# The opening of a fused DFT and gated-MLP kernel: one load queue for x, norm columns turned on the matmul engine, first weight folds moved ahead

## The chip, the core and the metric

The kernel runs on one core of a Trainium2 chip. The core has a matmul engine (TensorE, "PE" in the profile; its weight loads are shown apart as "PEld"), three engines for elementwise work (VectorE "DVE", ScalarE "ACT", GpSimd "POOL") and a synchronisation engine ("SP") that does little but issue transfers. 16 DMA engines move data between HBM and the core's memory (SBUF); transfers can be issued from SP, ACT and POOL, and each of these has a queue of its own. The matmul engine writes to PSUM, 2 KB banks per partition that DVE and ACT read and no transfer can reach. Everything is fp32, and a fp32 matmul instruction shows in the profile as two passes: 8 matmuls are listed as "x16".

The metric is the device time of one execution in microseconds.

## What is computed

```python
def _attn_ref(x):                       # x: (8, 3008, 256)
    X = np.fft.fft(x, axis=1)
    X = np.fft.fft(X, axis=2)
    return X.real

def _moe_ref(x, w_in, w_out):           # x: (24064, 256), w_in: (256, 2048), w_out: (2048, 256)
    h = x @ w_in
    g = h * np.cos(h)
    return g @ w_out
```

The output is `_moe_ref` of the real part of the 2-D transform.

## The kernel before

**The work.** 3008 = 47 x 64, so the transform along the sequence is done in two halves. The first half (`first_half`) multiplies by a 47-point DFT, for 4 columns i of the 64-column grid and their mirror columns at a time: eight chunks c = 0..7 per batch. Its results go to DRAM (`store_z`), come back turned (`load_z`), and the second half (`second_half`) multiplies by the other DFT and yields a group g of up to 256 tokens. The transform along the 256 channels is folded into `w_in`: `fold_weights(e, n)` multiplies 512 columns of `w_in` by the cosine (e = 0) or sine (e = 1) matrix, and `keep_fold` writes the result to `WC` or `WS`. One row of the sine fold, the "norm row", is kept apart by `keep_row` (`nrow[n]`); it is needed as a column, 128 values on 128 partitions, in `wn`.

**The steady state.** 8 batches x 6 groups x 8 pairs of hidden tiles make 384 steps. A step s has a `seed` (ACT writes `wn` column x `nb` + 0.25 into the PSUM tile H), two matmul groups `mm1(s, 0)` and `mm1(s, 1)` on top of it, rounding and sine on ACT, products on DVE, and 7 matmuls `mm2`. Steps are interleaved with a lag of 3 (`LAG`). `nb` is the group's norm row spread over 128 partitions; for all groups but the first it is made by two transfers on SP, `nd<-pq` (L530) and `nb<-nd` (L531), and the seeds of that group wait for it.

**The opening** (everything before the loop at L1018) is what the change is about. It is written out by hand: engines run their instructions in program order, and each of SP's, ACT's and POOL's transfers is issued in program order too.

- `load_x(p, c0, c1, side)` (L189-209) loads part of batch 0's x. Half p = 0 feeds chunks 0 to 3, p = 1 chunks 4 to 7; side 0 are the columns, side 1 the mirror columns. Each call is three transfers (16, 16 and 15 rows of the 47). Side 0 goes by SP; side 1 of p = 0 and the first half of side 1 of p = 1 go by ACT's queue, the rest by SP. One single column goes by POOL.
- SP and ACT share eight semaphores for their transfers in turn, so a transfer waits until the one eight before it has landed.
- `keep_busy(8, "H", 512)` (L904) runs 8 matmuls on constant data while x is on its way.
- `fold_chunk` (L297) makes sum and difference of x and its mirrored channels on DVE, with a small copy of channel 0 (L302) before them, in two buffers `xf0`. `middle(b, p)` (L335) transforms channel 128 for all 16 columns of half p at once; `DIRECT` = 7 is a chunk that PE folds itself, with twice the matmuls.
- The chunks run in the order 0, 1, 2, 3, 4, 5, 7, 6. The sine fold n = 0 is put before chunk 4 (L913-915), the cosine fold n = 0 and folds n = 1 after the last chunk, then `second_half(0, 0)`.
- `store_z(0, c, 0)` sends the near part of a chunk to DRAM: chunks 0 to 3 from POOL, later ones from SP, two of them from ACT. `load_z(0, 0)` waits for all eight chunks' near parts.
- `send_wn(n)` and `take_wn(n)` (L608-615) turn the norm row into a column: a transfer from SBUF to DRAM and one back, both on POOL's queue. Columns of n = 0 belong to steps 0 and 1 of each group (in the first group these use `seed_first`, a matmul on the row itself, instead); n = 1 serves steps 2 and 3, n = 2 steps 4 and 5, n = 3 steps 6 and 7.
- Loads of batch 1's x follow on SP (21 transfers, L180) and on POOL (7 transfers); then SP loads `xz` (L185) and only then comes to `nd` and `nb` of group 1.

The lines that the steps below touch: L302/L303 (chunk folds), L339/L346 (middle), L455/L440/L443 (first half), L577 (weight folds), L590/L594 (their copies by ACT), L598 (norm row), L610/L613 (norm column through DRAM), L627 (`keep_busy`), L660 (`seed`), L676 (`seed_first`), L690 (`mm1`), L780 (`mm2`), L507/L518/L522 (second half and its copies).

Of the kernel before, what the change touches and what calls it, by code (L numbers as in the profile page):

```python
# [11 lines left out]
FP = mybir.dt.float32  # L12
# [122 lines left out]
def kernel(  # L135
# [119 lines left out]
    nc.sync.dma_start(out=LCS, in_=LCS_dr.ap())  # L255
    nc.vector.memset(xs[0][:, 0:2048], 0.0)
# [12 lines left out]
    load_w(0)  # L269
# [27 lines left out]
    def fold_chunk(b, c, e):  # L297
# [3 lines left out]
        if e == 0:  # L301
            nc.vector.tensor_copy(out=fv[:, 0, :, 0], in_=xv[:, :, 0])  # L302
# [32 lines left out]
    def middle(b, p):  # L335
        xm = xs[p].rearrange("r (i d) -> r i d", d=ND)[0:XR, :, 128]
        pm = psum("pm", "M")[64:128, 0:XP]
        for i0, i1, q in ((0, 1, 2), (1, XP, 0)) if p == 0 else ((0, XP, 0),):
            nc.tensor.matmul(  # L339
                pm[:, i0:i1],  # L340
                lhsT=L[0:XR, 64 * q : 64 * q + 64],
                rhs=xm[:, i0:i1],
                start=True,
                stop=True,
            )
        nc.scalar.copy(out=mid[64:128, XP * p : XP * p + XP], in_=pm)  # L346
# [77 lines left out]
    def first_half(b, c):  # L424
# [3 lines left out]
        if c == 0:  # L428
            middle(b, 0)
# [70 lines left out]
    def second_half(b, g):  # L500
# [3 lines left out]
        pb = psum("pb")  # L504
        for q in range(4):
# [8 lines left out]
        pq = spool.tile([128, 512], FP, tag="pq", bufs=8, name="pq")  # L514
        pv = pq[:, 0 : 2 * T].rearrange("d (e t) -> d e t", e=2)
        bv = pb.rearrange("d (q e k) -> d e q k", q=4, e=2)
        if g == 0:
# [3 lines left out]
            edge = nc.scalar.copy if b else nc.vector.tensor_copy  # L521
            edge(out=pv[:, :, 192:225], in_=bv[:, :, 0, 0:33])  # L522
# [83 lines left out]
    wds = {}  # L606
# [96 lines left out]
    def dve_h(s):  # L703
        T = s.T
        s.h = spool.tile([128, 512], FP, tag="h", bufs=3, name="h")
        nc.vector.tensor_tensor(  # L706
# [221 lines left out]
    take_wn(1)  # L928
    fold(0, 1)
# [5 lines left out]
    for c in range(NCH):  # L935
# [6 lines left out]
    second_half(0, 0)  # L942
    combine_w2(2, 4)

    opening = {
        3: ((send_wn, 3), (take_wn, 3)),
# [9 lines left out]
    early = {3: (1, 3, "fft"), 5: (0, 3, "fft")}  # L956
# [12 lines left out]
    dve_h(s0)  # L969
# [8 lines left out]
    send_wn(2)  # L978
    take_wn(2)
# [10 lines left out]
    act_round(s1, 1)  # L990
    mm1(s2, 1)
# [17 lines left out]
    def beside(ins, ahead):  # L1009
        if ahead is not None:  # L1010
            tc.add_manual_dep(
                ins.ins,
                ahead.ins.name,
                mybir.DependencyInfo(mybir.DependencyClass.Sync, mybir.DependencyReason.DATA),
                reason="start with the PSUM reads",
            )

    for t in range(LAG, n + LAG + 1):  # L1018
        cur, prev, old, done = step(t), step(t - 1), step(t - 2), step(t - LAG)
        if cur:  # L1020
            mm1(cur, 0)
            act_e(cur)
            if t in early:
                fold(*early[t])
# [82 lines left out]
```

## Time and profile before

| | us |
|---|---|
| median of 3 runs | 1951.06 (1950.06 to 1951.55) |
| the profiled execution's own time | 1949.91 |
| its span, first to last instruction | 1948.1 |
| PE busy | 1929.5 |
| DVE busy | 1778.5 |
| ACT busy | 1528.7 |
| POOL busy | 397.8 |

The profile is of one execution; all its times are counted from the start of the span. The timeline lists instructions in order of time, those of one line merged: start, length, engine, line, operation, tiles written and read, count, and in brackets the idle time of the engine before it and what ended it. Times of a merged row reach from the first start to the last end. The view of windows gives, for a stretch, the busy time of each engine, the granted clock of PE (1.00 is full speed), the DMA engines' share and the GB/s moved. The chain of waits is followed back from the last instruction; 58% of it are L780 matmuls and 34% L690 matmuls.

### The profile page before, as it was taken

To read this page: it belongs to the slowest core of one execution; us is meant where nothing else is said; L and a number is where in the kernel's file an instruction comes from. 1 tells how busy PE (TensorE), PEld (TensorE's weight loads), DVE (VectorE), ACT (ScalarE), POOL (GpSimd) and SP (SyncE) were. 2 spreads that over 40 slices of the span, in tenths; PEclk is the share of its full clock that TensorE was granted. 3 is DMA by queue.
4 is the path that set the end of the run, shared out by engine and by line. 5 is a ranking of instruction groups with operands and counts; after the bars stand their busy time and mean duration, and the time that the engine had idled before them with its cause. 6 is when DMAs were issued, how large, how long until landed. Compare 5 with 4: busy or idle time off the path is not lost.

```text
span 1948.1 us, 30580 instructions
## 1 busy us (share of the span) xinstructions
PE 1929.5 (99%) x9546; PEld 1693.7 (87%) x9546; DVE 1778.5 (91%) x3343; ACT 1528.7 (78%) x2877; POOL 397.8 (20%) x468
## 2 busy tenths in 40 slices
PE   8999999999999999999999999999999999999998
PEld 3888899888998889988898888988889888898887
DVE  4899999999899998999989999899999999999998
ACT  3787878888788787888878788788877888788775
POOL 3322202222022211222112221122211222111101
PEclk9999999999999999999999999999999999999999
DMA  7321130012200121111211122111231100110000
GB/s 194 102 61 39 46 90 24 22 37 75 58 22 22 46 75 49 25 26 47 82 36 27 25 56 79 29 29 25 51 85 31 25 20 24 55 28 10 12 22 22
DMA packets 157804, 89.35 MB, mean 46 GB/s; under 512 B 106838, under 2 KB 152270, under 8 KB 155174
## 3 DMA queue, kind: packets, MB, share of 16 engines
q1 hardware_dynamic: 155331, 85.42, 16.6%
q10 hardware_dynamic: 1415, 1.27, 0.3%
q8 instruction: 76, 1.25, 0.3%
q0 software_dynamic: 896, 0.71, 0.2%
q14 instruction: 86, 0.70, 0.1%
HBM read 50.07 MB, written 37.28 MB: 45 GB/s over the span
## 4 chain that ended last, share of the span: by engine, by line
PE 96%; issue 1%; DMA 1%; DVE 1%; POOL 0%; SPq 0%; ACT 0%; ACTq 0%; DVEq 0%; POOLq 0%
PE M L780 58%; PE H L690 34%; PE pb L507 2%; PE pz L397 2%; DMA wn<-wd 0%; DMA xp<-in_x_dram 0%; PE pz L357 0%; DMA wd<-nrow 0%; SPq L887 0%; PE M L397 0%; POOL zd L487 0%; PE pz L385 0%; DVE r L735 0%; PE pz L455 0%; DVE S L746 0%
## 5 line engine op out<-in xcount | busy, mean ns | idle before, releaser
L780 PE MATMUL M<-S,VX 128*128 128x256 f32 (+1 forms) x2304 | 612.3, 375 | 0.0
L780 PEld LDWEIGHTS M<-S,VX 128*128 128x128 f32 x2304 | 437.8, 190 | 49.9
L721 ACT ACTIVATE r<-H 128x512 f32<-128x512 f32 (+1 forms) x384 | 226.1, 589 | 264.1 <-DVE h L706 262.5
L731 ACT ACTIVATE r<-r 128x1024 f32<-128x1024 f32 (+1 forms) x384 | 394.7, 1028 | 20.4 <-DVE r L725 16.2
L690 PE MATMUL H<-pq,WC 128*128 128x256 f32 (+1 forms) x1536 | 394.6, 379 | 2.0 <-ACT H L660 2.0
L690 PE MATMUL H<-pq,WS 128*128 128x256 f32 (+1 forms) x1536 | 389.6, 376 | 1.3 <-ACT ew L701 1.3
L780 PE MATMUL M<-r,w 128*128 128x256 f32 (+1 forms) x1536 | 387.7, 375 | 0.0
L660 ACT ACTIVATE H<-nb,wn 128x256 f32<-128x256 f32 (+1 forms) x764 | 362.0, 474 | 24.7 <-DMA wn<-wd 10.8
L706 DVE TENSOR_TENSOR h<-ew,H 128x512 f32<-128x512 f32 (+1 forms) x384 | 259.4, 676 | 101.9 <-PE H L690 69.1
L690 PEld LDWEIGHTS H<-pq,WC 128*128 128x128 f32 x1536 | 283.5, 190 | 52.8 <-ACT r L721 15.4
L780 PEld LDWEIGHTS M<-r,w 128*128 128x128 f32 x1536 | 300.1, 196 | 28.3 <-issue 0.9
L690 PEld LDWEIGHTS H<-pq,WS 128*128 128x128 f32 x1536 | 292.7, 191 | 35.6 <-ACT ew L701 2.3
L725 DVE SCALAR_TENSOR_TENSOR r<-r,H 128x512 f32<-128x512 f32 (+1 forms) x384 | 258.6, 674 | 34.5 <-ACT r L721 18.2
L701 ACT ACTIVATE ew<-H 128x512 f32<-128x512 f32 (+1 forms) x384 | 225.6, 588 | 53.1 <-PE H L690 44.4
L832 POOL TENSOR_TENSOR cb<-cb,mr 128x256 f32<-128x256 f32 (+3 forms) x188 | 158.0, 851 | 518.6 <-DVE S L756 484.0
L746 DVE TENSOR_TENSOR S<-r 128x512 f32<-128x512 f32 (+1 forms) x384 | 259.8, 676 | 0.1
L725 DVE SCALAR_TENSOR_TENSOR r<-r,h 128x512 f32<-128x512 f32 (+1 forms) x384 | 259.4, 676 | 0.0
L735 DVE SCALAR_TENSOR_TENSOR r<-H,r 128x512 f32<-128x512 f32 (+1 forms) x384 | 256.6, 668 | 2.3 <-ACT r L731 1.8
L735 DVE SCALAR_TENSOR_TENSOR r<-h,r 128x512 f32<-128x512 f32 (+1 forms) x384 | 258.4, 673 | 0.0
L721 ACT ACTIVATE r<-h 128x512 f32<-128x512 f32 (+1 forms) x384 | 236.0, 615 | 0.0
L316 POOL TENSOR_TENSOR xs<-xp 113x512 f32<-113x512 f32 x112 | 142.9, 1276 | 407.8 <-DVE S L756 405.3
L780 PE MATMUL M<-S,w 128*128 128x256 f32 (+1 forms) x768 | 225.5, 375 | 0.6 <-DVE S L756 0.6
(108 smaller groups left out, 1585.0 us busy)
## 6 DMA issues: line engine op xcount, KB each, us to landing
out_dram<-ob SPq DMA_DIRECT2D x728, 32.0 KB
xp<-in_x_dram SPq DMA_DIRECT2D x261, 56.0 KB
z<-zd SPq DMA_DIRECT2D x8, 1280.0 KB
zd<-zs SPq DMA_DIRECT2D x224, 40.0 KB
nb<-nd SPq DMA_DIRECT2D x40, 128.0 KB
zd<-zs SPq DMA_DIRECT2D x224, 8.0 KB
xp<-in_x_dram SPq DMA_DIRECT2D x54, 48.0 KB
xp<-in_x_dram SPq DMA_DIRECT2D x42, 49.0 KB
```

The lines of the kernel that those rows point to most:

```text
L316: return nc.gpsimd.tensor_tensor(out=xs2[e][0:XL], in0=xv[:, 0], in1=xv[:, 1], op=ALU.subtract if e else ALU.add,)
L660: nc.scalar.activation(out=s.H[:, u * T : u * T + T], in_=s.nb[:, 0:T], func=AF.Copy, bias=0.25, scale=wn[:, f : f + 1],)
L690: nc.tensor.matmul(s.H[:, u * T : u * T + T], lhsT=W[:, 128 * f : 128 * f + 128], rhs=s.pq[:, e * T : e * T + T], start=False, stop=True, ...
L701: nc.scalar.mul(out=s.ew[:, 0 : 2 * s.T], in_=s.H[:, 0 : 2 * s.T], mul=2.0)
L706: nc.vector.tensor_tensor(out=s.h[:, 0 : 2 * T].rearrange("p (u t) -> p u t", u=2)[:, :, ::-1], in0=s.ew[:, 0 : 2 * T].rearrange("p (u t) ...
L721: nc.scalar.activation(out=r, in_=h, func=AF.Copy, bias=BIG, scale=1.0)
L725: nc.vector.scalar_tensor_tensor(out=r, in0=r, scalar=-BIG, in1=h, op0=ALU.add, op1=ALU.subtract)
L731: nc.scalar.activation(out=r, in_=r, func=AF.Sin, bias=0.0, scale=SIN_SCALE)
L735: nc.vector.scalar_tensor_tensor(out=r, in0=h, scalar=-0.25, in1=r, op0=ALU.add, op1=ALU.mult)
L746: return nc.vector.tensor_tensor(out=sv[:, 0:2], in0=gv[:, 2:3].to_broadcast([128, 2, T]), in1=gv[:, 0:4:3], op=ALU.subtract,)
L780: nc.tensor.matmul(acc[key][m // 2][:, 256 * (m % 2) : 256 * (m % 2) + T], lhsT=w, rhs=a, start=first, stop=s.fp == 7, skip_group_check=True,)
L832: return nc.gpsimd.tensor_tensor(out=o, in0=a, in1=b, op=ALU.subtract if less else ALU.add)
```

## The change

It changes the opening in eleven places:

1. All of batch 0's x goes by SP's queue (the one single column stays on POOL). Side 0 is cut into pieces of 2 KB, no longer of 4 KB.
2. The load of `w_in`'s first 512 columns (`load_w(0)`) is issued right behind the constants, ahead of x.
3. `keep_busy` at the start is cut from 8 matmuls to 2; both folds n = 0 and the turning of their norm row follow at once, before chunk 0.
4. `send_wn` and `take_wn` are gone. `turn_row(n)` takes their place: four matmuls with the row's 128 values as weights and a single 1 as the moving operand, into a PSUM tile, and a copy of 4 columns to `wn` by DVE (n < 2) or ACT.
5. The channel-0 copies of the chunk folds leave DVE: chunks 0 to 3 on ACT, chunks 4 to 6 on POOL.
6. `middle` for the second half of x runs in two parts of 8 columns, before chunk 4 and before chunk 7.
7. The order of the chunks is 0, 1, 2, 3, 4, 7, 5, 6.
8. After the folds n = 1 and `turn_row(1)` one matmul on constant data is put ahead of `second_half(0, 0)`, and a half-length one behind it.
9. In `second_half(0, 0)` DVE's copy of the edge is placed behind the first of the four matmuls, ahead of ACT's copy.
10. `clear_later` (POOL's clearing of later buffers) comes after the first step's `dve_h` and waits for it.
11. `turn_row(2)` stands behind `mm1(s1, 1)`, `turn_row(3)` at step 4 behind `mm1(s4, 0)`.

POOL's program is then: stores of chunks 0 to 2, channel-0 copy of chunk 4, stores of chunk 3, channel-0 copies of chunks 5 and 6, the clearing, the 7 loads of batch 1's x.

```diff
     def load_x(p, c0, c1, side):
-        queue = nc.scalar if side and not c0 else nc.sync
...
-            load(nc.sync, 0, c0, c1, slice(i0 + c0, i0 + c1), max_dma_last_dim=4096)
+            load(nc.sync, 0, c0, c1, slice(i0 + c0, i0 + c1), max_dma_last_dim=2048)
...
-        load(queue, 3, c0 + skip, c1, slice(64 - i0 - c0 - skip, 64 - i0 - c1, -1))
+        load(nc.sync, 3, c0 + skip, c1, slice(64 - i0 - c0 - skip, 64 - i0 - c1, -1))
...
     nc.sync.dma_start(out=LCS, in_=LCS_dr.ap())
+    load_w(0)
...
-    load_w(0)
     for c0 in (0, XP // 2):
...
-    def clear_later():
-        nc.gpsimd.memset(xz, 0.0)
+    def clear_later(ahead):
+        beside(nc.gpsimd.memset(xz, 0.0), ahead)
...
-            nc.vector.tensor_copy(out=fv[:, 0, :, 0], in_=xv[:, :, 0])
+            edge = nc.scalar.copy if c < 4 else nc.gpsimd.tensor_copy
+            edge(out=fv[:, 0, :, 0], in_=xv[:, :, 0])
...
-    def middle(b, p):
+    def middle(p, c0, c1):
...
-        for i0, i1, q in ((0, 1, 2), (1, XP, 0)) if p == 0 else ((0, XP, 0),):
+        for i0, i1, q in ((0, 1, 2), (1, c1, 0)) if p == c0 == 0 else ((c0, c1, 0),):
...
+            if q == g == b == 0:
+                nc.vector.tensor_copy(out=pv[:, :, 192:225], in_=bv[:, :, 0, 0:33])
...
-    def send_wn(n):
-        wds[n] = dpool.tile([1, 512], FP, tag="wd", bufs=4, name="wd")
-        nc.gpsimd.dma_start(out=wds[n], in_=nrow[n][0:1, :])
-
-    def take_wn(n):
-        nc.gpsimd.dma_start(
-            out=wn[:, 4 * n : 4 * n + 4], in_=wds[n].rearrange("o (q p) -> (o p) q", p=128)
-        )
+    def turn_row(n):
+        pt = psum("pt")
+        for q in range(4):
+            nc.tensor.matmul(
+                pt[:, q : q + 1],
+                lhsT=nrow[n][0:1, 128 * q : 128 * q + 128],
+                rhs=ones[:, 0:1],
+                start=True,
+                stop=True,
+            )
+        take = nc.vector.tensor_copy if n < 2 else nc.scalar.copy
+        take(out=wn[:, 4 * n : 4 * n + 4], in_=pt[:, 0:4])
...
-    keep_busy(8, "H", 512)
-    order = [0, 1, 2, 3, 4, 5, DIRECT, 6]
+    keep_busy(2, "H", 512)
+    fold(1, 0, "H")
+    fold(0, 0, "H")
+    turn_row(0)
+    order = [0, 1, 2, 3, 4, DIRECT, 5, 6]
     folded = [c for c in order if c != DIRECT]
     chunk(folded.pop(0))
-    for k, c in enumerate(order):
-        if k == 4:
-            middle(0, 1)
-        if c != DIRECT and folded:
+    for c in order:
+        if c == 4:
+            middle(1, 0, XP // 2)
+        if c == DIRECT:
+            middle(1, XP // 2, XP)
+        elif folded:
             chunk(folded.pop(0))
-        if k == 4:
-            late = fold_weights(1, 0, "H")
-            keep_fold(*late)
         first_half(0, c)
         store_z(0, c, 0)
-    clear_later()
-    keep_row(*late)
-    fold(0, 0, "H")
     for s in steps[0:2]:
         fill_first(s)
-    send_wn(0)
-    take_wn(0)
+    fold(1, 1)
+    fold(0, 1)
+    turn_row(1)
     combine_w2(0, 2)
-    fold(1, 1)
-    send_wn(1)
-    take_wn(1)
-    fold(0, 1)
+    keep_busy(1, "M", 512)
     load_z(0, 0)
...
     second_half(0, 0)
+    keep_busy(1, "M", 256)
     combine_w2(2, 4)
...
-        3: ((send_wn, 3), (take_wn, 3)),
...
-    early = {3: (1, 3, "fft"), 5: (0, 3, "fft")}
+    early = {3: (fold, 1, 3, "fft"), 4: (turn_row, 3), 5: (fold, 0, 3, "fft")}
...
-    dve_h(s0)
+    clear_later(dve_h(s0))
...
-    send_wn(2)
-    take_wn(2)
...
+    turn_row(2)
     mm1(s2, 1)
```

More of the change, by code (lines that the diff above doesn't have):

```diff
@@ L345, in middle @@
             )
-        nc.scalar.copy(out=mid[64:128, XP * p : XP * p + XP], in_=pm)
+        nc.scalar.copy(out=mid[64:128, XP * p + c0 : XP * p + c1], in_=pm[:, c0:c1])
     def weights(q, r0, r1):
@@ L428, in first_half @@
         if c == 0:
-            middle(b, 0)
+            middle(0, 0, XP)
         fv = xf0[c % 2].rearrange("r (e c) -> r e c", e=2)
@@ L504, in second_half @@
         pb = psum("pb")
+        pq = spool.tile([128, 512], FP, tag="pq", bufs=8, name="pq")
+        pv = pq[:, 0 : 2 * T].rearrange("d (e t) -> d e t", e=2)
+        bv = pb.rearrange("d (q e k) -> d e q k", q=4, e=2)
         for q in range(4):
@@ L520, in second_half @@
             )
-            edge = nc.scalar.copy if b else nc.vector.tensor_copy
-            edge(out=pv[:, :, 192:225], in_=bv[:, :, 0, 0:33])
+            if b:
+                nc.scalar.copy(out=pv[:, :, 192:225], in_=bv[:, :, 0, 0:33])
         else:
@@ L705, in dve_h @@
         s.h = spool.tile([128, 512], FP, tag="h", bufs=3, name="h")
[L706 removed]
+        return nc.vector.tensor_tensor(
             out=s.h[:, 0 : 2 * T].rearrange("p (u t) -> p u t", u=2)[:, :, ::-1],
@@ L1007, in step @@
         return s if s is not None and (last is None or s.fp == 7) else None
[L1009 to L1016, printed above, removed]
     for t in range(LAG, n + LAG + 1):
@@ L1023 @@
             if t in early:
-                fold(*early[t])
+                early[t][0](*early[t][1:])
         if t - LAG - 1 == n - 1:
```

12 lines of the change are left out of this document (8 added, 4 removed).

## The prediction

> **What bounds the kernel now.** I read the busy shares, then the chain of waits, then the windows. The windows (stretch, its length, busy time of PE, PEld, DVE, ACT, POOL with counts, granted clock, DMA share, GB/s), cut where the stages change:
>
> ```profile
> 0.00:12.60 12.60, 9.00 (x17) 3.76 (x17) 4.21 (x6) 1.59 (x2) 7.46 (x13) 1.00 0.76 204
> ...
> 33.20:51.20 18.00, 15.00 (x47) 10.05 (x47) 6.25 (x14) 7.07 (x14) 1.82 (x3) 0.73 0.76 236
> ...
> 60.55:1941.00 1880.45, 1878.85 (x9388) 1666.78 (x9388) 1748.12 (x3281) 1505.65 (x2829) 376.95 (x428) 1.00 0.16 40
> ```
>
> From 60.55 on PE is busy 99.9% of the time at full clock, and the change touches almost nothing there. So what the opening saves reaches the end one for one, as long as nothing PE needs later arrives too late. Before 60.55 PE idles and, from 33.2 to 51.2, has a mean clock of 0.73. The chain (start, length, what), with its longest pieces there:
>
> ```profile
> 4.52 8.28 DMA xp<-in_x_dram
> ...
> 40.52 3.35 DMA wn<-wd
> ...
> 53.30 6.18 DMA wn<-wd
> ```
>
> These are x's last piece and two norm columns coming back from DRAM. Who suffers shows in the timeline, ACT first, then PE:
>
> ```profile
> 43.98 0.94 ACT L660 ACTIVATE H<-nb,wn 128x225 f32<-128x225 f32 x2 [6.23 <-DMA wn<-wd]
> ```
> ```profile
> 21.27 0.26 PE L339 MATMUL pm<-xp,LCS 110*64 110x16 f32 x2 [1.97 <-issue]
> 21.46 1.98 PE L577 MATMUL pw<-wr,LCS 128*128 128x512 f32 x4
> 23.37 1.94 PE L455 MATMUL pz<-xf,LCS 128*64 128x512 f32 x8
> ...
> 27.86 5.42 PE L577 MATMUL pw<-wr,LCS 128*128 128x512 f32 x12
> 33.22 1.13 PE L507 MATMUL pb<-BJ,z 128*128 128x128 f32 x8
> 35.18 1.02 PE L676 MATMUL H<-pq,nrow 1*128 1x225 f32 x4 [0.83 <-DVE pq L522]
> ...
> 39.05 3.18 PE L577 MATMUL pw<-wr,LCS 128*128 128x512 f32 x4
> ...
> 44.96 1.80 PE L690 MATMUL H<-pq,WC 128*128 128x225 f32 x4 [0.82 <-ACT H L660]
> 48.05 3.37 PE L690 MATMUL H<-pq,WS 128*128 128x225 f32 x8 [1.28 <-ACT ew L701]
> 51.21 2.23 PE L577 MATMUL pw<-wr,LCS 128*128 128x512 f32 x4
> ...
> 60.55 1.03 PE L690 MATMUL H<-pq,WC 128*128 128x225 f32 x4 [1.21 <-ACT H L660]
> ```
>
> The reader sees three things: the idle times in brackets, four fold passes taking 3.18 us where the twelve at 27.86 take 0.45 each, and the 1.97 us at 21.27, in which PE waits for the whole second half of x.
>
> **The change part by part.** All against the span of 1948.1.
>
> *Up to the first chunk.* PE now starts x with these:
>
> ```profile
> 3.60 9.07 PE L627 MATMUL pd<-VX 128*128 128x512 f32 x16 [3.60 <-DVE VX L258]
> ```
> ```profile
> 13.10 1.28 DVE L303 TENSOR_TENSOR xf<-xp 110x508 f32<-110x508 f32 x2
> ```
>
> At 0.45 a full-speed pass, 9.07 us for 16 passes means about four at double length. Two `keep_busy` matmuls (four passes) last to 7.2, the eight passes of both folds n = 0 to 10.8. ACT's and DVE's copies of the norm row fit behind the second fold. `turn_row` is not in the trace. Nearest by its 128 weight columns is L507, eight passes in 1.13 us; the top is eight passes at the 0.255 of L676, 2.0; the bottom eight at the 0.13 of L339, 1.0. I take 1.1: 11.9, and with DVE's copy of four columns 12.1. x must have landed by then. The sizes of the two transfers ahead of it:
>
> ```profile
> wr<-in_moe_w_in_dram SPq DMA_DIRECT2D x3, 512.0 KB
> ...
> LCS<-dft_L SPq DMA_DIRECT2D x1, 416.0 KB
> ```
>
> Before, 12.6 us moved 204 GB/s, 2.57 MB; now these two (0.95 MB) and x's first half (47 rows of 32 columns of 1 KB, 1.54 MB) make 2.5 MB in one queue, with the weights moving while x waits for its memsets. So about 12, and chunk 0's fold starts 1.0 us earlier. Bounds: 2.2 earlier if turning is free, and the slow case among the rivals.
>
> *The chunks.* Gone are the 1.97 us (`middle` in parts) and the sine fold at 21.46 (1.9 of its 1.98 us, which overlap the next). The new copies cost something. On POOL the copy for chunk 4 stands behind six stores:
>
> ```profile
> 20.21 1.09 POOL L487 DMA_DIRECT2D zd<-zs  x2 [0.16 <-ACT zs L461]
> ```
> ```profile
> 61.56 0.45 POOL L832 TENSOR_TENSOR VX<-VX,w 128x128 f32<-128x128 f32 x1
> ```
>
> Chunk 2's two stores take 1.09 us after its result is ready, the copy itself, at most as much as POOL's sum of a 128x128 tile (0.45) and at least nothing, 0.2. PE cannot begin chunk 4 before, and loses about 1.0 us. Behind that copy stand chunk 3's stores and chunk 5's copy; DIRECT, now between, covers them. ACT's copies for chunks 2 and 3 sit behind its result copies, but there DVE sets the pace (1.28 a chunk), so I cost them at nothing; without that cover each costs up to a wait for one result, 0.5. Sum so far: -1.0 - 1.97 - 1.9 + 1.0 = -3.9.
>
> *To the second half.* Twelve fold passes (5.42) become eight (3.6), one `turn_row` (1.1) and two dummy passes (0.9): +0.2. The data's way through DRAM shifts with the last result:
>
> ```profile
> 28.59 0.20 ACT L461 COPY zs<-mid 64x4 f32<-64x4 f32 x1
> ```
> ```profile
> 30.51 0.35 SPq L496 DMA_DIRECT2D z<-zd  x1
> ```
>
> z is asked for 1.72 us after the last copy ends and used from 33.22, so PE's 5.6 us and the transfers' way still end together, 3.7 earlier than before.
>
> *First steps.* `wn` no longer comes by DMA, so ACT's 6.23 us go, and with them PE's: the fold at 39.05 (3.18 to 1.8), the gap of 0.82, L690 at 44.96 (1.80 to 1.0), most of the gap of 1.28 (0.2 stays: PE still waits for `ew`), L690 at 48.05 (3.37 to 2.0), half of the 0.83 (edge copy earlier): -5.9. `turn_row(2)` adds 1.1: -4.8. The half clock goes because its gaps go; the windows that clock follows are these:
>
> ```profile
> 17.76:21.17 3.41, 1.54 (x5) 0.31 (x4) 2.95 (x7) 1.57 (x4) 3.10 (x6) 1.00 0.88 228
> ...
> 41.65:45.07 3.42, 2.60 (x11) 1.45 (x9) 0.00 (x0) 1.06 (x3) 0.00 (x0) 1.00 0.65 170
> 45.07:48.48 3.41, 2.12 (x5) 1.43 (x6) 2.64 (x5) 3.17 (x6) 0.52 (x1) 0.50 0.43 101
> ```
>
> A window with 0.82 us idle, much of the rest one-row matmuls, was followed by a halved one; one with 1.87 us idle was not. `turn_row` is one-row work too, so one halved window may return: 3.41 us at half speed cost up to 1.7.
>
> *Steps 3 and 4.* The 1.21 us at 60.55 and 0.4 of the fold at 51.21 go, `turn_row(3)` adds 1.1: -0.5. Sum on PE: -3.9 + 0.2 - 4.8 - 0.5 = -9.0.
>
> *What is late next.* SP's line, as it stands behind z (one row for its 21 loads), ACT and PE at the first step of group 1, and POOL's loads:
>
> ```profile
> 50.07 19.49 SPq L180 DMA_DIRECT2D xp<-in_x_dram  x21
> 69.81 3.00 SPq L185 DMA_DIRECT2D xz<-in_x_dram  x4
> 73.29 0.22 SPq L530 DMA_DIRECT2D nd<-pq  x1
> 74.39 0.36 SPq L531 DMA_DIRECT2D nb<-nd  x1
> ```
> ```profile
> 77.42 0.99 ACT L660 ACTIVATE H<-nb,wn 128x256 f32<-128x256 f32 x2
> ```
> ```profile
> 80.20 1.02 PE L690 MATMUL H<-pq,WC 128*128 128x256 f32 x4
> ```
> ```profile
> 54.08 3.54 POOL L180 DMA_DIRECT2D xp<-in_x_dram  x7
> ```
> ```profile
> SPq L530 <- ACT pq L524: 0.4, 1, 0.4
> ```
>
> SP finishes `xz` at 72.81 and issues `nd` 0.48 later, 0.4 of it (the last row, of the view of who waited for whom) for ACT: its line is full, and faster compute steps don't move it. It moves with z (-3.7). POOL's seven loads no longer wait for norm columns, so they run beside the far stores of z instead of beside SP's loads. That takes from the one what it gives to the other, up to their 3.54; with the norm column's transfers gone I put 0.7 in SP's favour (bounds -0.2 and 1.7), and the 0.4 for ACT goes. `nd` shifts by -4.8, the seed to 72.6, PE's L690 can start at 73.6: -6.6, where PE would be ready at 71.2. Behind that seed in ACT's order stand the sine of step 6 and the rounding of step 7, which PE needs a step later. So 2.4 us of idle appear; I take one halved window after them, +1.7.
>
> The Trainium skill, page "TensorE: Matmul & The Clock Gate", section "Part 1: The HAM clock gate", says that the clock halves after about one idle window of some 3.4 us. The rows above show a halving after far less idle time. By the rule the stall of 2.4 us would leave the clock alone, and the sum would be -6.6; the forecast's own range holds that.
>
> Sum: -6.6 + 1.7 = -4.9, a span of 1943.2. The profiled execution took 1949.91, 1.15 under the median; against the median, 1951.06 - 4.9 = 1946.2.
>
> **The rivals.** *SP's line has room*, so that all of PE's gain stays: -9.0 or a little more, 1942.0. For it: ACT showed no wait at 77.42, and POOL's loads leave SP's way. Against: SP had 0.48 us to spare ahead of `nd`, no more.
>
> *The front gains little.* Turning costs 2.0 each instead of 1.1 (+0.9 before chunk 0, which z and SP's line inherit), a halved window falls among the chunks and POOL's copies hold chunk 5 too (+1.5 together, an estimate from the 1.7 of a halved window and the 1.09 of two stores, half hidden). Then z comes 1.5 earlier, and SP's line gives -1.5 - 1.1 - 1.8 (PE's slack behind the seed) + 1.7: 1948.4, no change that can be told. (About 0.2%, 3.9 us, is what a measurement of this kernel tells from none.)
>
> *One queue is too slow for x.* This one ends slower. The loads' cost of issue on SP and ACT:
>
> ```profile
> L197 SPq DMA_DIRECT2D xp<-in_x_dram x12: 577/716/960, 3.1 to 17.3; - x12
> ```
> ```profile
> 3.10 7.74 ACTq L197 DMA_DIRECT2D xp<-in_x_dram  x6
> ```
> ```profile
> 7.30 10.82 SPq L197 DMA_DIRECT2D xp<-in_x_dram  x9
> ```
>
> At SP's median of 0.716, eighteen loads go out from 3.10 to 16.0. At ACT's 1.29 with its waits they end at 26.3, and the last lands as long after its issue as before (18.12, the last row's end, to PE's start at 21.27), at 29.4. Then come two chunks (1.94, by the row at 23.37), DIRECT with as many matmuls as two (1.9), the results' copies (0.9, from the folds' start at 27.86 to 28.79) and the 1.72: z is late by 5.5, and SP's line with it, -1.1 - 1.8 and the halved window's 1.7 make +4.3: 1955.4. It decides from about 0.8 us a load on, where the last part becomes later than chunk 4's end, and turns the change into a loss at about 1.05. Against it: the cost above; for it: in the stretch to 12.60 two queues were at work and the DMA share was only 0.76.
>
> **How the numbers follow.** Forecast 0.52, its own range 1943.9 (no halved window, -6.6, and 0.6 more from SP) to 1948.0 (0.9 for SP's lower bound, 0.9 for dear turning); SP's line has room 0.24; front gains little 0.13; one queue too slow 0.11. The range takes in the second and third: 1941.0 (the second, with turning nearly free) to 1949.5 (the third, with SP's line at its lower bound). Faster by over 0.2% (under 1947.2): 0.24 and four fifths of 0.52, 0.66; slower 0.11; the rest 0.23.
>
> **What would show it.** Chunk 0's fold at 12.1; z asked for near 26.7; no "DMA wn" at all; L577 at full speed in the first steps; the seed of group 1's first step late, with "DMA nb" as the releaser, and SP without a pause before `nd`. A PE gap there under 1 us would prove SP's line wrong; a chunk 0 later than 13.1 the first part; a late `middle` wait the queue.

## The result, and the profile after

| | before | after |
|---|---|---|
| median of 20 runs each, us | 1951.14 (1949.14 to 1953.80) | 1947.43 (1945.52 to 1949.71) |
| the profiled execution's own time | 1949.91 | 1947.28 |
| its span | 1948.1 | 1945.5 |

The ratio is 0.9981 (95% interval 0.9975 to 0.9988): 3.7 us faster by the medians, 2.6 by the two profiled executions. The forecast was 4.9.

Line numbers in the changed kernel are 2 to 4 higher: L579 are the weight folds, L611 `turn_row`, L664 the seeds, L694 `mm1`, L784 `mm2`, L532/L533 `nd` and `nb`. The windows of the changed kernel, two cut as before and two of the clock's own, 3.41 us long (busy time of PE, PEld, DVE, ACT, POOL with counts, granted clock, DMA share, GB/s):

```profile
0.00:12.60 12.60, 9.00 (x22) 4.29 (x22) 5.05 (x8) 2.86 (x4) 7.45 (x13) 1.00 0.87 234
33.20:51.20 18.00, 17.80 (x75) 12.91 (x75) 9.75 (x20) 11.02 (x23) 3.91 (x11) 1.00 0.65 203
...
73.34:76.75 3.41, 1.44 (x6) 1.02 (x7) 0.71 (x3) 1.96 (x5) 1.26 (x1) 1.00 0.07 22
76.75:80.16 3.41, 3.41 (x10) 3.03 (x9) 3.41 (x8) 3.17 (x7) 0.00 (x0) 0.50 0.00 0
```

The 1.00 of the first row holds from 8.48 on, where the record of the clock begins; the four passes of `keep_busy` ahead of that take 0.95 us each and not 0.45. From 33.2 to 51.2 PE went from 15.0 to 17.8 us busy, and from a clock of 0.73 to 1.00. In place of that a new hole opened: 1.97 us idle in the window from 73.34, and the next at half clock. PE's timeline shows both, with the steps of the prediction ahead of them:

```profile
7.17 4.25 PE L579 MATMUL pw<-wr,LCS 128*128 128x512 f32 x8
11.35 1.05 PE L611 MATMUL pt<-ones,nrow 1*128 1x1 f32 x8
...
20.28 1.08 PE L455 MATMUL pz<-xf,LCS 128*64 128x512 f32 x4 [1.29 <-POOL xf L302]
...
44.04 1.88 PE L579 MATMUL pw<-wr,LCS 128*128 128x512 f32 x4
...
51.67 1.00 PE L694 MATMUL H<-pq,WC 128*128 128x225 f32 x4
...
73.17 0.66 PE L784 MATMUL M<-S,w 128*128 128x225 f32 x2 [0.76 <-DVE S L760]
75.80 1.18 PE L694 MATMUL H<-pq,WC 128*128 128x256 f32 x4 [1.97 <-ACT H L664]
76.77 1.71 PE L784 MATMUL M<-r,w 128*128 128x225 f32 x4
...
81.98 1.02 PE L694 MATMUL H<-pq,WC 128*128 128x256 f32 x4
```

Against the same instructions before, the fold at 44.04 is 7.2 us earlier (51.21), the first matmul of step 4 at 51.67 8.9 (60.55), group 1's first matmul at 75.80 only 4.4 (80.20), and the first matmul of the step after it at 81.98 2.6 (84.59). SP's timeline says why:

```profile
3.10 13.48 SPq L196 DMA_DIRECT2D xp<-in_x_dram  x18
...
27.99 0.35 SPq L496 DMA_DIRECT2D z<-zd  x1
...
48.13 0.34 SPq L496 DMA_DIRECT2D z<-zd  x1
...
50.98 16.80 SPq L180 DMA_DIRECT2D xp<-in_x_dram  x21
67.90 1.93 SPq L185 DMA_DIRECT2D xz<-in_x_dram  x4
69.93 0.23 SPq L532 DMA_DIRECT2D nd<-pq  x1
71.74 0.36 SPq L533 DMA_DIRECT2D nb<-nd  x1
```

The near part of z is asked for 2.5 us earlier than before (30.51), its far part 0.7 later (47.42), `nd` 3.4 earlier (73.29). ACT's seed of group 1 waits for what follows from it:

```profile
74.75 0.99 ACT L664 ACTIVATE H<-nb,wn 128x256 f32<-128x256 f32 x2 [4.81 <-DMA nb<-nd]
```

DVE's timeline explains the 0.76 in brackets at 73.17, and shows the start of the chunks:

```profile
12.91 1.29 DVE L303 TENSOR_TENSOR xf<-xp 110x508 f32<-110x508 f32 x2 [0.31 <-DMA xp<-in_x_dram]
...
72.52 0.29 DVE L326 TENSOR_TENSOR xfz<-xz 113x127 f32<-113x127 f32 x1 [1.49 <-DMA xz<-in_x_dram]
```

DVE waits for `xz`, also a load of SP's line, and PE for DVE.

### The profile page after: what moved, and what is told of

Its sections match the earlier page's. It is cut to its first block, busy times and chain, and to the rows that moved or that the text cites. A ratio compares the mean times of both kernels' runs of the same rounds, so it can differ in the third digit from the quotient of the medians.

```text
span 1945.5 us, 30633 instructions
## 1 busy us (share of the span) xinstructions
PE 1927.9 (99%) x9572; PEld 1695.0 (87%) x9572; DVE 1777.3 (91%) x3338; ACT 1529.7 (79%) x2884; POOL 393.1 (20%) x463
## 4 chain that ended last, share of the span: by engine, by line
PE 97%; SPq 1%; DVE 1%; DMA 0%; issue 0%; ACT 0%; POOL 0%; DVEq 0%; POOLq 0%; ACTq 0%
PE M L784 58%; PE H L694 34%; PE pb L510 2%; PE pz L397 2%; SPq L196 1%; PE pw L579 1%; PE pz L357 0%; SPq L891 0%; PE M L397 0%; PE pt L611 0%; DMA nb<-nd 0%; PE pz L455 0%; DMA BJ<-dft_B 0%; PE pz L385 0%; DVE r L739 0%
## 5 line engine op out<-in xcount | busy, mean ns | idle before, releaser
L784 PE MATMUL M<-S,VX 128*128 128x256 f32 (+1 forms) x2304 | 612.7, 375 | 0.0
L784 PEld LDWEIGHTS M<-S,VX 128*128 128x128 f32 x2304 | 438.1, 190 | 50.0
L694 PE MATMUL H<-pq,WC 128*128 128x256 f32 (+1 forms) x1536 | 393.7, 379 | 2.0 <-ACT H L664 2.0
L784 PE MATMUL M<-r,w 128*128 128x256 f32 (+1 forms) x1536 | 388.6, 375 | 0.0
L694 PE MATMUL H<-pq,WS 128*128 128x256 f32 (+1 forms) x1536 | 388.1, 375 | 0.1
L664 ACT ACTIVATE H<-nb,wn 128x256 f32<-128x256 f32 (+1 forms) x764 | 362.0, 474 | 20.5 <-DMA nb<-nd 4.8
L694 PEld LDWEIGHTS H<-pq,WC 128*128 128x128 f32 x1536 | 283.1, 190 | 52.5 <-ACT r L725 15.8
L784 PEld LDWEIGHTS M<-r,w 128*128 128x128 f32 x1536 | 300.6, 196 | 28.3 <-issue 0.7
L694 PEld LDWEIGHTS H<-pq,WS 128*128 128x128 f32 x1536 | 291.7, 190 | 34.0 <-ACT ew L705 0.6
L784 PE MATMUL M<-S,w 128*128 128x256 f32 (+1 forms) x768 | 225.8, 375 | 1.3 <-DVE S L760 1.3
```

The costliest lines, as they stand in the source:

```text
L664: nc.scalar.activation(out=s.H[:, u * T : u * T + T], in_=s.nb[:, 0:T], func=AF.Copy, bias=0.25, scale=wn[:, f : f + 1],)
L694: nc.tensor.matmul(s.H[:, u * T : u * T + T], lhsT=W[:, 128 * f : 128 * f + 128], rhs=s.pq[:, e * T : e * T + T], start=False, stop=True, ...
L784: nc.tensor.matmul(acc[key][m // 2][:, 256 * (m % 2) : 256 * (m % 2) + T], lhsT=w, rhs=a, start=first, stop=s.fp == 7, skip_group_check=True,)
```

## The experiments

Twelve kernels were timed, each against the kernel before on the same chip. "Changed" is the changed kernel alone, "+nb" the changed kernel with the edit of the first experiment. The gains named below are differences of medians, often of different sets of runs. The kernel before itself has medians from 1951.14 to 1952.92 in these sets, and by the ratios, which set each kernel against its own set, such a difference comes out up to 3 us another way (e1 lies 4.3 us below the changed kernel by them, not 2.4). Where intervals overlap, times alone do not decide, and the traces have to.

| experiment | median, us | ratio to before, interval |
|---|---|---|
| changed kernel | 1947.43 | 0.9981 (0.9975 to 0.9988) |
| e1 changed, nb of group 1 by PE | 1944.98 | 0.9959 (0.9947 to 0.9972) |
| e2 before, nb of group 1 by PE | 1951.45 | 0.9996 (0.9987 to 1.0005) |
| e3 changed, nd and nb on POOL's queue | 1945.04 | 0.9962 (0.9949 to 0.9974) |
| e4 changed, dummy matmuls in the hole | 1947.14 | 0.9973 (0.9962 to 0.9984) |
| e5 changed, POOL's x loads later | 1944.86 | 0.9968 (0.9956 to 0.9979) |
| e6 +nb, norm columns by DMA | 1946.42 | 0.9973 (0.9963 to 0.9982) |
| e7 +nb, x on two queues | 1947.31 | 0.9980 (0.9971 to 0.9989) |
| e8 +nb, channel-0 copies all on ACT | 1943.57 | 0.9967 (0.9955 to 0.9979) |
| e9 e8 and e5 together | 1943.98 | 0.9959 (0.9947 to 0.9972) |
| e10 as e9, nd and nb on POOL | 1944.60 | 0.9963 (0.9951 to 0.9976) |
| e11 as e10, 128-row products | 1942.90 | 0.9951 (0.9937 to 0.9964) |
| e12 as e9, 128-row products | 1941.82 | 0.9946 (0.9932 to 0.9959) |

**Is it SP's line? e1, e2, e3.** e1 and e2 make the same edit to the two kernels:

```diff
-        if b == 0 and g == 0:
+        if b == 0 and g < 2:
             return
         nd = dpool...
...
-    def spread_norm():
-        T = _width(0)
-        pq, nb = ready[0, 0]
-        pn = psum("pn", "M")
+    def spread_norm(g=0, tag="M"):
+        T = _width(g)
+        pq, nb = ready[0, g]
+        pn = psum("pn", tag)
...
         5: ((second_half, 0, 1),),
+        6: ((spread_norm, 1, "fft"),),
```

> The changed kernel, but the norm row of the second group (group 1) is spread over the partitions by one matmul against ones and a VectorE copy a step later, as group 0's already is, instead of by the two transfers nd and nb on SP's line. Theory (SP's line sets the first step of group 1): that step's first matmul, at 75.80 in the changed kernel after 1.97 us of idle, starts when PE is ready, at 73.83 plus 0.4 to 0.5 us for the added matmul, so near 74.3; the 0.76 us wait for VectorE ahead of it stays, as it hangs on the xz loads; the halved clock window at 76.75 goes, worth another 1.7; so 3 to 3.5 us off 1947.4, near 1944. Rival (the front gained little, and PE would be no earlier): the added matmul costs 0.5 us, 1947.9.

> The kernel before with the same single edit (norm row of group 1 by matmul and copy, no nd and nb). Theory: in the kernel before PE reached that step about when nb had landed (80.20), so nothing is gained but what the added matmul costs and a small wait gives: 1950.5 to 1951.7; and the difference to the changed kernel with the same edit shows what the front gained on PE, 7 to 7.6 us, of which nb had swallowed half. Rival (nb held both kernels alike): this kernel too becomes about 3 us faster, and the difference to the changed kernel stays near 3.7.

PE in e1, then in e2 (there L690 is `mm1`; the added matmul takes 0.69 us in both):

```profile
74.39 0.66 PE L784 MATMUL M<-S,w 128*128 128x225 f32 x2 [0.48 <-DVE S L760]
74.88 1.03 PE L694 MATMUL H<-pq,WC 128*128 128x256 f32 x4
75.75 0.93 PE L784 MATMUL M<-r,w 128*128 128x225 f32 x4
```
```profile
80.83 1.03 PE L690 MATMUL H<-pq,WC 128*128 128x225 f32 x4
```

In e1 group 1's first matmul follows without a wait and the four after it run at full clock (0.93, not 1.71): 2.4 us off, a little less than expected. The kernel before gains nothing from the same edit. With `nb` out of the way the two kernels, in one set of runs, lie 6.5 us apart (1951.45 and 1944.98), a little less than the 7 to 7.6 expected; as they were, 3.7. So the front had won some 2.8 us more than the result shows, and the wait for `nb` swallowed that. (e2's profiled execution was its longest, so no other row of it is used.)

e3 keeps the transfers and changes only the queue:

```diff
+        queue = nc.gpsimd if b == 0 and g == 1 else nc.sync
-        nc.sync.dma_start(out=nd...
-        nc.sync.dma_start(out=nb...
+        queue.dma_start(out=nd...
+        queue.dma_start(out=nb...
```

> The changed kernel with group 1's nd and nb issued on POOL's queue instead of SP's, nothing else moved. Theory (it is the place in SP's line that is late, not the transfer): POOL can issue nd soon after pq is copied, near 66 to 67, nb lands near 71, and the first step of group 1 starts when PE is ready (73.8), with no halved window: 1943.5 to 1944.5. Rival (the transfers are slow because 25 loads of x run beside them, whatever the queue): nb still lands after 74 and the time stays within 0.7 us of 1947.4.

PE in e3 (L695 is `mm1`):

```profile
74.75 1.13 PE L695 MATMUL H<-pq,WC 128*128 128x256 f32 x4 [0.49 <-ACT H L665]
```

The wait shrinks from 1.97 to 0.49 and the time by 2.4 us, to half a microsecond above the range expected. Most of the wait was the place in SP's line and not the transfers themselves; the 0.49 that stays is still a wait for `nb`, which POOL could issue only at 70.40, when `nd` (66.14) had landed.

**What the halved window costs, e4.**

```diff
         if cur:
+            if t == 8:
+                keep_busy(3, "fft", 256)
             mm1(cur, 0)
```

> The changed kernel with three dummy matmuls of 256 columns put on PE just ahead of group 1's first matmul, where PE idled 1.97 us; they feed nothing. Theory (the idle stretch there halves the clock in the window that begins near 76.75): the wait for nb stays, the matmul still starts at 75.8, but the clock stays full and L784's four after it take about 0.95 us and not 1.71; the kernel is 1.5 to 1.7 us faster, near 1945.8. Rival (the clock falls for another reason, such as the one-row matmuls or the power): the window is halved again and the time is unchanged, or up to 0.5 us longer.

The windows, PE and DVE of e4:

```profile
73.34:76.75 3.41, 2.19 (x10) 1.62 (x9) 0.08 (x1) 1.94 (x5) 0.43 (x1) 1.00 0.12 16
76.75:80.16 3.41, 3.34 (x17) 2.82 (x16) 3.41 (x8) 3.19 (x7) 0.00 (x0) 1.00 0.00 0
```
```profile
75.81 1.13 PE L694 MATMUL H<-pq,WC 128*128 128x256 f32 x4 [1.22 <-ACT H L664]
76.78 0.93 PE L784 MATMUL M<-r,w 128*128 128x225 f32 x4
...
87.37 1.13 PE L694 MATMUL H<-pq,WC 128*128 128x256 f32 x4
```
```profile
76.67 0.63 DVE L739 SCALAR_TENSOR_TENSOR r<-H,r 128x450 f32<-128x450 f32 x1 [3.77 <-ACT r L735]
...
90.99 0.69 DVE L710 TENSOR_TENSOR h<-ew,H 128x512 f32<-128x512 f32 x1 [1.13 <-PE H L694]
```

The clock stays at 1.00 and the four matmuls behind the first take 0.93, as the theory says, but the median falls by 0.3 us and not by 1.6. (By the ratio it would be 1.6; the intervals overlap, so the trace has to decide.) The first matmul of group 1 starts where it did, and at 87.37 PE is 0.6 ahead of the changed kernel (88.01); at the end the span is 0.5 shorter (1945.0 against 1945.5). That the dummy matmuls kept the clock up is not shown by this alone: in e4 the clock's windows fall at other times (71.57, 74.99, 78.40), so that the wait is split between two of them. Between its two bracketed waits, from 76.67 to 89.86, DVE works without a pause. It folds batch 1's columns in these steps beside its own work, so it sets the pace there, with the half clock or without it.

**POOL's loads, e5.**

```diff
-                at(max(o + k, LAG) if b == 1 and k else o + k, load_later_x, ...
+                at(max(o + k, LAG) if b == 1 else o + k, load_later_x, ...
```

> The changed kernel with POOL's seven x loads of the second batch given one step later, behind POOL's sums of step 3 (near 56 us instead of 38.1), so that they no longer run beside SP's far stores of z. Theory (these loads hold back the far stores and with them SP's line): SP's load of z-far, 48.13 in the changed kernel, comes 1 to 2 us earlier, the 21 x loads, nd and nb follow, group 1's first matmul starts 1 to 1.5 us before 75.8, and the time falls by 1 to 2 us. Rival (the far stores take their time by themselves, or the loads now collide with SP's 21 loads instead): z-far within 0.5 us of 48.1, or earlier with nd no earlier, and the time within 0.7 us of the changed kernel.

SP in e5:

```profile
28.17 0.35 SPq L496 DMA_DIRECT2D z<-zd  x1
...
45.50 0.34 SPq L496 DMA_DIRECT2D z<-zd  x1
...
48.47 17.02 SPq L180 DMA_DIRECT2D xp<-in_x_dram  x21
...
67.98 0.23 SPq L532 DMA_DIRECT2D nd<-pq  x1
```

From z's near to its far part it takes 17.3 us instead of 20.1, and `nd` comes 2.0 earlier. 2.6 us faster: more than expected, and as much as taking `nb` off the line. The loads, now issued from 55.17 on, cost SP's 21 loads hardly anything (17.02 against 16.80).

**The parts of the front, e6 to e8, on top of e1.** e6 brings back the two transfers per norm column:

```diff
     def turn_row(n):
-        pt = psum("pt")
-        ...
+        wds[n] = dpool.tile([1, 512], FP, tag="wd", bufs=4, name="wd")
+        nc.gpsimd.dma_start(out=wds[n], in_=nrow[n][0:1, :])
+        nc.gpsimd.dma_start(out=wn[:, 4 * n : 4 * n + 4], in_=wds[n].rearrange(...))
```

> On the kernel with the norm row of group 1 by matmul (1944.98 us): the four norm columns again by the kernel before's two transfers each (row to DRAM, columns back, on POOL's queue), at the places where the one-row products stand; the folds stay ahead of x. Theory (the transfers' round trip, 6 to 10 us in the kernel before, sits on the path): the column of n=1, whose row is made near 28 to 29, comes back at 36 to 40, so the seed of step 2 (37.0 with the products) waits up to 3 us; that of n=2 (row near 40.8, POOL's seven x loads around it) comes near 50 to 53, when seed 4 needs it near 49; PE idles and the clock halves once or twice: 1946 to 1949. Rival (with the folds ahead of x the round trip is covered, and the products only cost PE 1.05 us each): 1 to 2 us faster, 1943 to 1944.

ACT in e6 (L660 are the seeds):

```profile
38.96 0.94 ACT L660 ACTIVATE H<-nb,wn 128x225 f32<-128x225 f32 x2 [4.09 <-DMA wn<-wd]
...
52.65 0.94 ACT L660 ACTIVATE H<-nb,wn 128x225 f32<-128x225 f32 x2 [2.54 <-DMA wn<-wd]
```

The waits are there, the first longer than the 3 us expected, but the clock does not fall; 1.4 us is the price by the medians (the intervals overlap). The products, four times 1.05 us of PE, look worth it.

e6 also shows what the norm columns' transfers do to SP's line. SP's 21 loads of batch 1 in e1, then in e6, where two of the columns go through DRAM beside them:

```profile
51.74 16.98 SPq L180 DMA_DIRECT2D xp<-in_x_dram  x21
```
```profile
47.79 20.81 SPq L180 DMA_DIRECT2D xp<-in_x_dram  x21
```

They take 3.8 us longer. POOL's seven loads run beside them too in e6, but in e5 these alone made 17.02.

e7 puts x back on two queues:

```diff
+        queue = nc.scalar if side and not c0 else nc.sync
...
-            load(nc.sync, 0, ..., max_dma_last_dim=2048)
+            load(nc.sync, 0, ..., max_dma_last_dim=4096)
...
-        load(nc.sync, 3, c0 + skip, ...
+        load(queue, 3, c0 + skip, ...
```

> On the kernel with the norm row of group 1 by matmul (1944.98 us): x again as in the kernel before, side 1 of the first part on ACT's queue and in pieces of 4 KB on SP's. Theory (what bounds the landing of x is the transfers and not the number of queues; and ACT, which issues them, is late for its copies of the first folds): the first chunk folds within 0.5 us of where it does with one queue (12.7 to 12.9), and the time is within 0.7 us. Rival (one queue is 0.8 us too slow, since x's last piece came at 12.5 where the folds would have let it start at 12.1): up to 0.8 us faster.

ACT, then PE in e7 (L612 is `turn_row`):

```profile
3.10 7.89 ACTq L197 DMA_DIRECT2D xp<-in_x_dram  x6
...
12.53 0.66 ACT L593 ACTIVATE WS<-pw,mask 128x512 f32<-128x512 f32 x1
```
```profile
13.95 1.86 PE L612 MATMUL pt<-ones,nrow 1*128 1x1 f32 x8 [3.21 <-DVE nrow L601]
```

Neither expectation held: 2.3 us slower, and no run of e7 is as fast as the slowest of e1. ACT is stuck issuing until 11.0, copies the first fold at 12.53 (9.74 in the changed kernel), and PE waits 3.21 us for the norm row and turns it at half clock, which lasts to 20.77, far into the chunks. x itself lands no later: its last piece comes at 12.58 by the trace's semaphores, at 12.51 in the changed kernel. So the single queue brings x no sooner; it frees ACT, which the folds ahead of x need for their copies. Parts 1 and 3 of the change are one.

e8 takes the copies off POOL:

```diff
-            edge = nc.scalar.copy if c < 4 else nc.gpsimd.tensor_copy
-            edge(out=fv[:, 0, :, 0], in_=xv[:, :, 0])
+            nc.scalar.copy(out=fv[:, 0, :, 0], in_=xv[:, :, 0])
```

> On the kernel with the norm row of group 1 by matmul (1944.98 us): the channel-0 copies of the chunks from 4 on by ACT as those before, none on POOL. Theory (chunk 4's copy sits behind six stores on POOL, and PE waits 1.34 us for it): that wait goes, the later chunks, z's load and everything behind come 0.9 to 1.3 us earlier, near 1943.9. Rival (VectorE, which folds back to back at 1.2 us a chunk, takes the wait over, or ACT's copies come later by its own work): less than 0.4 us.

z is asked for at 26.91 instead of 28.66 in e1. That is not all the copy's: e1's profile has a halved window among the chunks (from 13.62), e8's and the changed kernel's have none. Against the changed kernel (27.99, with chunk 0 begun 0.1 earlier) it is 1.2. The median falls by 1.4 us, but the ratio does not (0.9967, e1 0.9959) and the intervals overlap: the trace shows the gain, the times do not. Two of the six runs took 1947.4 and 1948.4, and the profile has a halved window later on:

```profile
32.43:35.84 3.41, 3.21 (x14) 2.18 (x14) 0.99 (x3) 0.89 (x3) 0.00 (x0) 1.00 0.99 328
35.84:39.26 3.42, 3.42 (x7) 1.55 (x5) 1.78 (x3) 1.77 (x4) 1.55 (x7) 0.50 0.71 209
```

The window ahead of it has only 0.2 us of idle, but about half of its work (1.02 and 0.64 us) are products of one row.

**Together, e9 to e12.** e9 joins e1, e5 and e8; e10 has e3's edit in place of e1's; e11 and e12 give the one-row products of group 0 (and, in e12, group 1's norm row) 128 rows, 127 of them zero weights:

```diff
+    nc.gpsimd.memset(nrow[0], 0.0)
+    nc.gpsimd.memset(first, 0.0)
+    nc.gpsimd.memset(first[0:1], 1.0)
...
-        nc.tensor.matmul(pn[:, 0:T], lhsT=ones, rhs=pq[0:1, T : 2 * T], ...
+        nc.tensor.matmul(pn[:, 0:T], lhsT=first, rhs=pq[:, T : 2 * T], ...
...
-                lhsT=nrow[0][0:1, ...
-                rhs=s.pq[0:1, T : 2 * T],
+                lhsT=nrow[0][:, ...
+                rhs=s.pq[:, T : 2 * T],
```

> The changed kernel with three edits together: the norm row of group 1 by matmul and copy, POOL's seven x loads one step later, and all channel-0 copies by ACT. Theory (SP's line, the loads that slowed it and POOL's copy each held something back): z-near is asked near 26.9 to 27.2, z-far near 44.5, VectorE no longer waits for xz, and what is left is PE's and VectorE's own work: 1942 to 1943.5, a little below the 1943.57 us of the kernel without the later loads. Rival (with nb off SP's line the loads' place is worth nothing): 1943.6 or above.

> The same, but group 1's nd and nb on POOL's queue instead of the matmul and the copy. Theory (SP's line): nb lands near 70, before PE is ready, and PE is spared the 0.63 us of the matmul and VectorE, which is full in steps 8 to 10, the 0.42 us of the copy: 0.4 to 0.6 us faster than with the matmul, 1941.5 to 1943. Rival (POOL's loads, now just ahead of nd in its queue, make nb late again): PE waits for nb up to 1 us and the time is that of the matmul's kernel or above.

> The same as the last one, with the one-row products of group 0's first two steps and of its norm row (1.02, 1.02 and 0.64 us of PE) given 128 rows, the other 127 of the weights zero: same results, columns and number of matmuls, so the same PE time; POOL clears the added zeros before 12 us. Theory (a stretch of one-row products looks idle to what grants the clock: the window before the halved one near 35.6 in the last profile held 1.66 us of them and hardly 0.2 us of idle): no halved window between 32 and 43, and no runs 4 us above the fastest as the kernel with ACT's copies had (1942.8 to 1944.1 four times, 1947.4 and 1948.4); median 0 to 2 us lower. Rival (rows do not matter, only idle time does): the same windows and spread as the last one, within 0.5 us.

> The four edits that stood their test, in one kernel: norm row of group 1 by matmul and copy (now with 128 rows too), POOL's seven x loads a step later, channel-0 copies by ACT, 128 rows in the products of group 0's norms. Theory (their gains add as far as PE and VectorE allow): no halved window from 5 us on, no wait for nb or xz, the first matmul of group 1 near 72.9 to 73.2; VectorE stays full in steps 8 to 10 and sets the pace there; 1942 to 1943, at least 4 us below the changed kernel's 1947.43, and with a narrow spread. Rival (VectorE's extra copy takes back what the wait for nb cost): the same as with nb on POOL's queue, 1942.9 or above.

e9 gains nothing on e8 by the median, so the rival has it: with `nb` off SP's line the loads' place is worth nothing that these runs can tell. e10 is no faster than e9. In its profile PE comes to group 1 late, at 77.08, and does not wait for `nb`. In e11, which keeps that queue, it waits 0.86 us there. That is not the rival's reason, POOL's loads: `nd` is issued at once, at 64.64, and `nb` at 68.73, when `nd` has landed; the two transfers just take that long. The windows of e10, then those of e12:

```profile
28.40:31.82 3.42, 2.42 (x14) 1.68 (x13) 1.82 (x6) 0.59 (x1) 0.00 (x0) 1.00 0.89 259
31.82:35.23 3.41, 3.41 (x11) 2.67 (x12) 1.52 (x4) 0.48 (x1) 0.00 (x0) 0.50 0.91 293
35.23:38.64 3.41, 3.41 (x9) 1.89 (x7) 0.00 (x0) 0.55 (x1) 0.00 (x0) 0.50 0.80 260
38.64:42.06 3.42, 3.42 (x7) 2.18 (x7) 1.02 (x3) 1.49 (x4) 0.42 (x4) 0.50 0.65 188
```
```profile
27.87:31.29 3.42, 2.51 (x13) 1.64 (x12) 1.79 (x6) 0.59 (x1) 0.00 (x0) 1.00 0.84 264
31.29:34.70 3.41, 3.33 (x11) 2.81 (x12) 1.55 (x5) 0.48 (x1) 0.00 (x0) 0.50 0.92 287
34.70:38.11 3.41, 3.16 (x15) 2.49 (x14) 0.82 (x2) 1.45 (x3) 0.00 (x0) 1.00 0.75 244
```

Both lose the clock after a window with 0.9 to 1.0 us of idle, in which `turn_row(1)` runs too (and both had lost it once before, among the chunks, from 14.75 and 14.22). With one-row products behind it the clock stays down for three windows, though PE is busy all through; with 128-row products it is back after one. e11 had no halved window in the opening, and its five runs lie within 1.2 us (e10: 3.3). That fits the theory. These two runs alone do not show it, since the windows fall at other places in every execution (the last section counts them over all profiles); and e12's expectation of no halved window at all did not hold for its profiled execution. That one was its longest, 1944.64; the other four took 1941.44 to 1941.87. Its span, 1941.4, is only 1.3 to 1.7 above theirs. By the median e12 is 5.6 us below the changed kernel, and its interval lies wholly below the changed kernel's: it beats both.

## Why the prediction was right, and where its sizes were off

**The course of events was right.** PE's gain reaches the first step of group 1, SP's line comes too late with `nb`, PE idles there (2.4 forecast, 1.97 measured, and 0.76 for `xz` that I had not seen), and one halved window follows. e1 and e3 show that it is the line, e2 that it did not bind before. The rival "SP's line has room" falls with them. From 81.98 on the lead of 2.6 stays to the end, so what the opening saves does reach it one for one. The sizes were worse than the medians make them look. In the two profiled executions the gain is 2.6 and not 4.9, and on SP's path, which decides, every term was off the same way: z by 1.2, the line behind it by 0.3, `nd` by 0.7, the halved window by 0.1. That the medians came within 1.2 (1947.43 against 1946.2) is partly luck: the profiled execution of the kernel before lies 1.2 below its median, that of the changed kernel 0.15.

**Chunk 0: the first term that failed.** I had x landing near 12 and the fold at 12.1, 1.0 earlier. It began at 12.91, 0.2 earlier than before. `turn_row` was right (1.1 forecast, 1.05 measured), but the twelve passes ahead of it ended at 11.35 and not at 10.8. ACT and DVE in the changed kernel:

```profile
12.61 0.30 ACT L302 COPY xf<-xp 110x4 f32<-110x4 f32 x2 [0.56 <-DMA xp<-in_x_dram]
```
```profile
12.44 0.16 DVE L619 COPY wn<-pt 128x4 f32<-128x4 f32 x1 [1.29 <-PE pt L611]
```

x was there for ACT's copy at 12.61, and DVE was free at 12.60: the two limits met, both half a microsecond late. The 0.31 that the profile puts to x in DVE's row at 12.91 is something else, for in e5 x was there at 12.24 (ACT's copy of it), DVE was free at 12.78, and it began 0.31 later again; meanwhile it works off a wait for one semaphore after the other. As for x, in the first 12.6 us 2.95 MB moved (234 GB/s), not the 2.5 that I had summed: at SP's 0.75 us a load, pieces of x's second half were being issued from about 7.6 on; that they took x's share is likely and not shown.

**The chunks.** From chunk 0's fold to the end of the last result's copy it now takes 13.4 us, before 15.7: -2.3 where I had -2.9. The end of the chunks on ACT in the changed kernel, and POOL's copy for chunk 4:

```profile
24.93 0.54 ACTq L487 DMA_DIRECT2D zd<-zs  x1
...
26.13 0.20 ACT L461 COPY zs<-mid 64x4 f32<-64x4 f32 x1
```
```profile
19.73 0.50 POOL L302 COPY xf<-xp 110x4 f32<-110x4 f32 x1
```

PE waited 1.29 for the latter instead of 1.0 (0.50 against my 0.2); e8 got 1.2 back by removing it. Yet up to PE's last matmul of the chunks they are 2.8 shorter, about as summed. What is missing is lost behind PE, in a term that I had left out: ACT issues a store (0.54) between its last two results, and its last copy ends 1.42 after that matmul (24.91); in the kernel before it was 0.86 (27.93). So z came 2.5 earlier, not 3.7. (By my own terms it should have been 3.9: the 0.2 of PE's folds stands behind the chunks, and z does not wait for it.)

**First steps and steps 3 and 4** were sized well: 7.2 - 2.5 = 4.7 (4.8 forecast) to the fold at 44.04 if counted from z, 5.1 from PE's second half (31.13 against 33.22), and `mm2` behind `turn_row(3)`, at 53.58 instead of 61.42, adds 0.7 (0.5). PE's sum is -7.8, not -9.0; the 1.2 missing are z's.

**SP's line.** I let POOL's seven loads take from the far stores what they give back to SP's loads. e5 corrects that: beside the far stores they cost 2.8 us (20.1 - 17.3), beside SP's 21 loads 0.7 at most (from z's far part to `nd` 22.5 us with them, 21.8 without). That the forecast for the line behind z (-1.1) came near the measured -0.8 is luck: the far stores' part grew by 3.2 (16.9 to 20.1), and the rest, 25.9 us before, shrank by 4.1. For that rest I had put 0.7 in SP's favour with the norm columns' transfers gone, and 0.4 for ACT; e6 shows what mattered: with these transfers the 21 loads take 3.8 longer. `nd` then needed 1.8 us to `nb`'s issue, and not the 1.1 of before. With z's 1.2 and the 0.3 that makes the seed of group 1, at 74.75, 2.2 later than my 72.6.

**The halved window** came, and from 75.80 to 81.98 the lead fell by 1.8, as the 1.7 had it. But e4 shows that this is not its price: without it, DVE takes all but 0.5 to 0.6 of that by the traces, all but 0.3 by the medians. I had looked at PE and SP there, not at DVE, which is full in steps 8 to 10.

**The clock.** The window ahead of the halved one had 1.97 us of idle, in e8's profile 0.2 and in e10's 1.0, of 3.41 each. The Trainium skill, page "TensorE: Matmul & The Clock Gate", section "Part 1: The HAM clock gate", gives one idle window as the condition; these rows halve long before: by the rule the clock would have stayed up and the forecast been -6.6. The same section says that the window runs freely and so falls differently in each run; the boundaries at 31.82 in e10 and 31.29 in e12 agree, and so does the first full clock, granted from 8.48 in the changed kernel and from 6.72 in e4, which do the same up to there.

**The other rivals.** "One queue is too slow" did not come: SP's eighteen loads went out in 13.48 us, 0.75 each, under the 0.8 from which it would have begun to cost, and e7 shows that the second queue would have cost more. "The front gains little" needed z only 1.5 earlier; it was 2.5. One of its conditions, a halved window among the chunks, is missing from the changed kernel's profile but stands in six others with the same front (e1, e3, e4, e9, e10 and e12, from between 13.5 and 14.8). In e1, e3 and e4 z is then asked for 16.2 to 16.4 us after chunk 0's fold begins, here 15.1, and only 1.7 to 2.0 earlier than before. So this rival was nearer than one profile shows.

## What to carry to other kernels

When a front part gets faster, follow every queue to its next deadline: here 2.8 us, more than two fifths of what PE had won, went into a 1 KB row that stood behind 25 loads, and moving it to an idle queue or to one matmul gave back 2.4. A shortened stall is worth only what the next engine leaves of it, so look at what is full right behind (DVE, in e4) before pricing it. And two parts of a change can be one: a queue that is no faster may still be what frees the engine that another part needs.

## What the hardware showed unexpectedly

- Matmuls of one weight row counted like idle time for PE's clock. I cut the first 95 us of the 14 kept profiles into windows at the clock's own changes (3.41 us each); 343 of them began at full clock. In 320, idle time and one-row products (where no other matmul ran beside them) made less than 1.6 us together, and the clock fell behind none; with 1.6 to 1.87 us it fell behind 4 of 11, with 1.89 or more behind all 12. Idle time alone does not sort them: 0.20 us in e8 was followed by a fall, 1.87 in the kernel before (from 17.76) was not. Behind a halved window the clock stayed down after 0.95 us or more of the two (5 windows) and came back after 0.51 or less. That fits the 10.2 us at half clock in e10 while PE was busy 100%. This is a count over runs, not an experiment on this alone.
- The same products with 128 rows took no longer (1.03 and 0.92 us for four passes in e11, against 1.02).
- Seven loads on POOL's queue beside SP's stores of small pieces cost SP's line 2.8 us; beside loads of x 0.7 at most. Two norm columns sent through DRAM beside those loads cost most of 3.8 us (e6).
- A copy of 110 x 4 values took 0.50 us on POOL, 0.20 on ACT and 0.17 on DVE (in the kernel before); what it cost PE, 1.29 us, was mostly the stores in front of it.
